# Turning batch 0's queries behind both probes of the first token, with small products among the warming ones

## The chip, the cores and the metric

The kernel runs on one core of a Trainium2 chip. The metric is the device time of one execution in microseconds (us), where lower is better. Times of the kernel before are the median of three runs; the profile comes from one further execution.

## What is computed

Eight batches, eight heads, 576 tokens, head width 64. First, 32 packs per head attend to the keys and values, and the queries then attend to the packed result; second, each batch's tokens go through a two-layer expert network (512 to 1024 to 512 wide), whose expert is chosen by a gate:

```python
def sm_attn(qq, kk, vv):
    s = scale * np.matmul(qq, kk.transpose(0, 1, 3, 2))
    a = np.exp(s - np.max(s, axis=-1, keepdims=True))
    a = a / (np.sum(a, axis=-1, keepdims=True) + 1e-09)
    return np.matmul(a, vv)
p_packed = sm_attn(p, k, v)
x = sm_attn(q, p_packed, p_packed)        # heads side by side: (8, 576, 512)
# per token: expert e by argmax of x @ w_gate, or the one before it by w_local
h = np.maximum(x[b, s] @ w1[e], 0.0)
out[b, s] = p[e] * (h @ w2[e])
```

## The kernel before

The kernel takes one expert for a whole batch, that of its first token, and works through the eight batches one behind the other; other experts, where a token has strayed, are done by a general branch at the end. For each batch the packs and keys (`turn_keys`) and queries (`turn_queries`) are turned so that the head width lies on the partitions, `scores` and `keys` compute the packed attention, and `queries` (for batch 0 `first_queries`) the second attention. `pack_weights` multiplies the expert's first-layer weights by the packed values (line 1190), so that layer 1 (`layer1`, line 1218) works on the attention shares directly; a product in single precision is split into a high and a low half on each side (wph and wpl, a2h and a2l, h and its rest, w2s) and done in three parts. Layer 2 (`layer2`, line 1271) adds up eight chunks of 128 hidden units for five blocks of tokens: three products make one group of a block and a chunk.

Batch 0 has a way of its own, since nothing is there to hide it. Before any load is there, `keep_warm` issues products on zeros (line 228), five of 256 columns by the list `WARM`, and more of them wherever the planner sees TensorE wait before the first layer. Packs are turned (line 425), then keys (line 451, six groups of three turns of 128 columns), then the packs' scores are taken (line 459). When the two halves of the packed values (ppT) are there, `early_choice` finds the expert of the first token alone: two probes (line 987, one per half of the heads), an exponential on ScalarE (line 1004), the turned shares on VectorE (et, line 1011), and their product with the gate (line 1020), which needs the gate weights that line 950 makes and line 959 copies on ScalarE. Its largest entry is the expert; SyncE reads it into a register, and only then are this expert's weights loaded: w1k (the first half of layer 1 in two pieces), four pieces of layer 2, and w1t, the second half of layer 1. The queries of batch 0 (load at line 292, turned at line 451, copied out of PSUM at line 452 by ScalarE, one of six by VectorE) are needed for the second attention of all its tokens, at line 459 again.

What order all this takes is set by a planner (`weave`): every stage is a generator that yields `need(...)`, a condition on tiles, banks of PSUM and flags; `Clock` estimates when each is ready; and the first thread that is ready by that estimate is let on, the layers' thread (`chunks`) behind the others. The order is fixed when the program is built, and each engine then runs its own list in order. So a condition that changes at one place also moves what the planner puts into the stretch behind it. A bank of PSUM is handed out by `bank`, the one that is free soonest.

## Time and profile before

| | us |
|---|---|
| median of 3 runs | 407.37 |
| lowest and highest of these | 407.05, 409.86 |
| the profiled execution | 410.66 |
| its span, first to last instruction | 408.9 |

The five engines are TensorE (PE, its weight loads apart as PEld), VectorE (DVE), ScalarE (ACT), GpSimd (POOL) and SyncE (SP, which issues the loads). A timeline row gives the start, the time that it covers, and the count of its instructions; products in fp32 stand there as two passes each, those of the layers as one. In the order's rows below, a product counts once.

### The profile page before, as it was taken

The numbers are of one execution on the slowest core, as the hardware profiler recorded it, in microseconds if no ns is written. First come the engines' busy times: TensorE is split into PE (matmuls) and PEld (weight loads), VectorE is DVE, ScalarE is ACT, GpSimd is POOL, SyncE is SP. The second block draws the span as 40 slices with busy tenths as digits, with TensorE's granted clock in tenths as the row PEclk, the third lists the DMA queues.
The fourth block names the chain that finished last, engine by engine and source line by source line (L and its number), as shares of the span: only waits on it lengthen the run. The fifth ranks groups of instructions, "written<-read, shape, count | busy, mean of one in ns | idle before, by whom it ended". The sixth has DMA issues, their size and how long they took to land.

```text
span 408.9 us, 10974 instructions
## 1 busy us (share of the span) xinstructions
PE 396.4 (97%) x4267; PEld 318.3 (78%) x4268; DVE 263.1 (64%) x755; ACT 179.8 (44%) x423; POOL 110.2 (27%) x139
## 2 busy tenths in 40 slices
PE   8888999999999999999999999999999999999994
PEld 7656877788786888778877788778878788778883
DVE  3677657778788877576776688439863695332221
ACT  2564733644337642294315741545343642453121
POOL 1006600812036313054303521234303422323000
PEclk9999999999999999999999999999999999999998
DMA  7889799990999999849996996699693104910102
GB/s 221 247 281 271 108 132 334 205 222 27 154 249 276 232 148 214 320 145 165 181 313 219 162 195 228 240 171 174 151 328 113 65 0 138 325 44 22 54 0 70
DMA packets 183133, 73.02 MB, mean 179 GB/s; under 512 B 158949, under 2 KB 162085, under 8 KB 182949
## 3 DMA queue, kind: packets, MB, share of 16 engines
q1 hardware_dynamic: 182932, 72.15, 74.2%
q8 instruction: 35, 0.57, 0.6%
q14 instruction: 22, 0.17, 0.1%
q10 hardware_dynamic: 144, 0.13, 0.1%
HBM read 62.82 MB, written 9.44 MB: 177 GB/s over the span
## 4 chain that ended last, share of the span: by engine, by line
PE 89%; DMA 6%; SPq 1%; DVE 1%; issue 1%; ACT 0%; ACTq 0%
PE bank L1271 44%; PE bank L1218 25%; PE bank L1275 4%; PE bank L1190 4%; PE bank L1279 4%; DMA w1t<-in_moe_w_dram 3%; DMA raw<-in_q_dram 2%; PE bank L569 2%; PE bank L764 2%; PE bank L521 2%; DMA raw<-in_k_dram 1%; PE bank L1039 1%; SPq L1149 1%; PE bank L587 0%; DVE wpl L1202 0%
## 5 line engine op out<-in xcount | busy, mean ns | idle before, releaser
L1271 PE MATMUL bank<-w2s,h 128*128 128x512 f32 (+1 forms) x792 | 202.1, 390 | 0.0
L1271 PEld LDWEIGHTS bank<-w2s,h 128*128 128x128 f32 x792 | 138.3, 188 | 28.0 <-issue 4.0
L1250 POOL TENSOR_TENSOR w2s<-w2raw,w2s 128x512 fp32r<-128x512 f32 (+1 forms) x68 | 83.3, 1244 | 146.9 <-ACT w2s L1246 114.5
L1233 DVE SCALAR_TENSOR_TENSOR h<-bank,h 128x256 fp32r<-128x256 f32 x192 | 61.1, 347 | 80.7 <-ACT h L1229 80.4
L1229 ACT ACTIVATE h<-bank 128x320 fp32r<-128x320 f32 (+1 forms) x128 | 52.7, 412 | 126.3 <-PE bank L1218 125.6
L1218 PEld LDWEIGHTS bank<-a2h,wph 128*128 128x128 f32 x256 | 46.1, 188 | 18.2 <-issue 5.9
L1218 PE MATMUL bank<-a2h,wph 128*128 128x256 f32 (+1 forms) x256 | 56.8, 303 | 0.0
L1218 PE MATMUL bank<-a2h,wpl 128*128 128x256 f32 (+1 forms) x256 | 55.0, 296 | 0.2 <-DVE wpl L1202 0.2
L1218 PE MATMUL bank<-a2l,wph 128*128 128x256 f32 (+1 forms) x256 | 55.0, 296 | 0.0
L1246 ACT CAST w2s<-w2raw 128x512 fp32r<-128x512 f32 x64 | 39.0, 619 | 8.9 <-DMA w2raw<-in_moe_w_dram 8.5
L1218 PEld LDWEIGHTS bank<-a2h,wpl 128*128 128x128 f32 x256 | 41.0, 188 | 0.4 <-DVE wpl L1202 0.4
L1218 PEld LDWEIGHTS bank<-a2l,wph 128*128 128x128 f32 x256 | 40.9, 189 | 0.0
L827 POOL TENSOR_TENSOR a2l<-a2t,a2h 128x320 fp32r<-128x320 f32 (+1 forms) x26 | 20.7, 817 | 65.7 <-ACT a2h L821 65.7
L1202 DVE TENSOR_TENSOR wpl<-bank,wph 128x512 fp32r<-128x512 f32 (+1 forms) x34 | 21.2, 652 | 13.4 <-ACT wph L1199 13.3
L1199 ACT CAST wph<-bank 128x512 fp32r<-128x512 f32 (+1 forms) x34 | 17.4, 566 | 22.3 <-PE bank L1190 22.2
L1275 PE MATMUL bank<-w2s,h 128*128 128x512 f32 x64 | 25.9, 404 | 0.0
L1279 PE MATMUL bank<-w2s,h 128*64 128x512 f32 x64 | 25.2, 393 | 0.0
L1310 ACT ACTIVATE o<-bank,pe 128x512 f32<-128x512 f32 x23 | 15.5, 700 | 12.4 <-PE bank L1271 12.4
L751 DVE STREAM_TRANSPOSE qn<-qn 128x1152 f32<-128x1152 f32 x14 | 19.0, 1363 | 0.0
L1190 PE MATMUL bank<-w1t,ppT 64*32 64x512 f32 x240 | 16.3, 601 | 1.6 <-DMA w1t<-in_moe_w_dram 1.6
L472 DVE STREAM_TRANSPOSE qn<-qn 128x1152 f32<-128x1152 f32 x12 | 16.2, 1353 | 0.0
L1275 PEld LDWEIGHTS bank<-w2s,h 128*128 128x128 f32 x64 | 12.0, 188 | 5.3 <-issue 3.2
(166 smaller groups left out, 382.7 us busy)
## 6 DMA issues: line engine op xcount, KB each, us to landing
w2raw<-in_moe_w_dram SPq DMA_DIRECT2D x64, 256.0 KB, 7.7
w1t<-in_moe_w_dram SPq DMA_DIRECT2D x15, 1024.0 KB, 7.1
qn<-in_q_dram SPq DMA_DIRECT2D x28, 288.0 KB, 4.5
out_dram<-o SPq DMA_DIRECT2D x31, 256.0 KB, 2.5
kv<-in_v_dram SPq DMA_DIRECT2D x24, 288.0 KB, 6.5
qn<-in_k_dram SPq DMA_DIRECT2D x24, 288.0 KB, 4.6
raw<-in_k_dram SPq DMA_DIRECT2D x4, 576.0 KB, 4.8
kv<-in_v_dram SPq DMA_DIRECT2D x4, 560.0 KB, 9.5
```

The source lines that it names most:

```text
L751: nc.vector.transpose(out=qT, in_=qT)
L827: engine.tensor_tensor(out=a2l[:, cols], in0=a2t[:, cols], in1=a2h[:, cols].bitcast(F32), op=ALU.subtract)
L1190: nc.tensor.matmul(out=ts[Q][32 * h:32 * h + 32, :width], lhsT=packs_of(st, rows, Q, h), rhs=w1t[rows, h], start=True, stop=True,)
L1202: nc.vector.tensor_tensor(out=lo[:, Q, cols], in0=ts[Q][:, :width], in1=hi[:, Q, cols].bitcast(F32), op=ALU.subtract,)
L1218: nc.tensor.matmul(out=t[:, :width], lhsT=st["wp"][c // 4][wi][:, Q, fs], rhs=a2[ai][Q][:, ts], start=(n == 0), stop=(n == 5),)
L1229: nc.scalar.activation(out=h[:, :n], in_=t[:, :n], func=AF.Relu)
L1233: nc.vector.scalar_tensor_tensor(out=h[:, dst:dst + z - a], in0=t[:, a:z], scalar=0.0, in1=h[:, a:z].bitcast(F32), op0=ALU.max, op1=ALU.su ...
L1246: nc.scalar.copy(out=w[:, 0], in_=raw)
L1250: rest.tensor_tensor(out=w[:, 1, cols], in0=raw[:, cols], in1=w[:, 0, cols].bitcast(F32), op=ALU.subtract)
L1271: nc.tensor.matmul(out=acc, lhsT=hs[hi], rhs=w[:, wi, cols], start=(c == 0 and n == 0), stop=(c == NC - 1 and n == 2),)
L1275: nc.tensor.matmul(out=acc, lhsT=h[:, EDGE:EDGE + 2 * TAIL], rhs=w[:, 0], start=(c == 0), stop=False, skip_group_check=True,)
L1279: nc.tensor.matmul(out=acc[0:TAIL], lhsT=h[:, EDGE:EDGE + TAIL], rhs=w[:, 1], start=False, stop=(c == NC - 1), skip_group_check=True,)
```

## The change

The list `WARM` loses one of its five wide products, and twenty-nine products of 32 columns on 64 rows come ahead of it, on the four column groups of the array in turn. `turn_queries` of batch 0 waits until both probes are issued, not only the first. Everything else that moves is moved by the planner.

```diff
--- before.py
+++ after.py
@@ -42,7 +42,7 @@
 
 FIRST_BACKLOG = 1400.0
 
-WARM, FILL, EACH = (256,) * 5, 0.8, 1.8
+WARM, SHORT, FILL, EACH = (256,) * 4, 29, 0.8, 1.8
 
 LAT, SAME = 160.0, 127.0
 START, FIRST_LOAD = 6100.0, 1700.0
@@ -227,6 +227,9 @@
             at_, n = (0, n) if aside_[0] is warm_ps else (HALF, n * 7 // 8)
             nc.tensor.matmul(out=aside_[0][:, at_:at_ + n], lhsT=warm[:, :128], rhs=warm[:, :n], start=True, stop=True)
 
+    for n in range(SHORT):
+        g = 32 * (n % 4)
+        nc.tensor.matmul(out=warm_ps[g:g + 32, :32], lhsT=warm[:64, g:g + 32], rhs=warm[:64, :32], start=True, stop=True)
     keep_warm(*WARM)
     clock.until["PE"], clock.until["DMA"] = START, FIRST_LOAD
 
@@ -741,7 +744,7 @@
     def turn_queries(st, Q):
         if st["early"]:
             if Q == 0:
-                yield need(when=lambda: st.get("probed", 0) > 0)
+                yield need(when=lambda: st.get("probed", 0) > 1)
                 act, dve = nc.scalar.copy, nc.vector.tensor_copy
                 yield from turn_whole(st, "q", (act, act, act, dve, act, act))
             return
```

The first place is TensorE from the first probe of the first token on. Here `ppT,q` are the probes, `wgl,ppT` the gate weights, `ident,raw` a group of turns (of batch 0's queries down to the row with `gate`, and of batch 1's keys behind the row with `p_in`), `qT,ppT` the scores of batch 0's queries. Before:

```order
L987 MATMUL bank_124<-ppT,q_88 32x32 x4
L451 MATMUL bank_306<-ident,raw 128x128 x3
L987 MATMUL bank_124<-ppT,q_88 32x32 x4
L950 MATMUL bank_315<-wgl,ppT 32x32 x8
L228 MATMUL bank_66<-warm 128x128
L451 MATMUL bank_335<-ident,raw 128x128 x3
L451 MATMUL bank_340<-ident,raw 128x128 x3
L451 MATMUL bank_345<-ident,raw 128x128 x3
L451 MATMUL bank_350<-ident,raw 128x128 x3
L1020 MATMUL bank_124<-gate_90,et 1x32 x2
L451 MATMUL bank_361<-ident,raw 128x128 x3
L425 MATMUL bank_397<-ident,p_in 128x128 x2
```

After (all lines behind the added ones are three higher):

```order
L990 MATMUL bank_152<-ppT,q_116 32x32 x8
L953 MATMUL bank_337<-wgl,ppT 32x32 x8
L454 MATMUL bank_347<-ident,raw 128x128 x3
L454 MATMUL bank_361<-ident,raw 128x128 x3
L454 MATMUL bank_366<-ident,raw 128x128 x3
L454 MATMUL bank_372<-ident,raw 128x128 x3
L454 MATMUL bank_377<-ident,raw 128x128 x3
L454 MATMUL bank_382<-ident,raw 128x128 x3
L1023 MATMUL bank_152<-gate_118,et 1x32 x2
L228 MATMUL bank_66<-warm 128x128
L462 MATMUL bank_394<-qT,ppT 32x6x16x3 x4
L462 MATMUL bank_399<-qT,ppT 32x6x16x3 x4
```

The probes and gate weights stand ahead of all query turns now, the sixth group of these comes ahead of the logit product (line 1020, now 1023), and the scores of batch 0 come ahead of batch 1's packs and keys.

At the same place on ScalarE: the copies of ppT and of the query turns, the exponential of the first token (`es,em`) and the copy of the gate weights. Before:

```order
L736 COPY ppT<-bank_298 128x128
L452 COPY qT<-bank_306 128x384
L1004 ACTIVATE es,em<-es,em 128x32
L959 COPY gate_90<-bank_315 128x64
L452 COPY qT<-bank_335 128x384
L452 COPY qT<-bank_340 128x384
L452 COPY qT<-bank_350 128x384
L452 COPY qT<-bank_361 128x384
L429 COPY p_in<-bank_397 128x256
```

After:

```order
L739 COPY ppT<-bank_326 128x128
L455 COPY qT<-bank_347 128x384
L1007 ACTIVATE es,em<-es,em 128x32
L455 COPY qT<-bank_361 128x384
L455 COPY qT<-bank_366 128x384
L962 COPY gate_118<-bank_337 128x64
L455 COPY qT<-bank_377 128x384
L455 COPY qT<-bank_382 128x384
L432 COPY p_in<-bank_453 128x256
```

The first query copy stays ahead of the exponential; the gate copy goes from the row behind the exponential to the third row behind it.

The second place is TensorE around the products that need w1t. Of the layer-2 rows (`w2s,h`) two stand for each chunk, one for each of the first two token blocks: a bank for each block. Before:

```order
L1271 MATMUL bank_574<-w2s,h 128x512 x3
L1271 MATMUL bank_583<-w2s,h 128x512 x3
L1218 MATMUL bank_590<-a2h,wph 128x256 x2
L1218 MATMUL bank_590<-a2h,wpl 128x256 x2
L1218 MATMUL bank_590<-a2l,wph 128x256 x2
L1190 MATMUL bank_608<-w1t,ppT 32x512 x4
L1190 MATMUL bank_609<-w1t,ppT 32x512 x4
L1271 MATMUL bank_574<-w2s,h 128x512 x3
L1271 MATMUL bank_583<-w2s,h 128x512 x3
L1271 MATMUL bank_574<-w2s,h 128x512 x3
L1271 MATMUL bank_583<-w2s,h 128x512 x3
L1218 MATMUL bank_643<-a2h,wph 128x256 x2
```

After:

```order
L1274 MATMUL bank_600<-w2s,h 128x512 x3
L1274 MATMUL bank_609<-w2s,h 128x512 x3
L1221 MATMUL bank_616<-a2h,wph 128x256 x2
L1221 MATMUL bank_616<-a2h,wpl 128x256 x2
L1221 MATMUL bank_616<-a2l,wph 128x256 x2
L1274 MATMUL bank_600<-w2s,h 128x512 x3
L1193 MATMUL bank_641<-w1t,ppT 32x512 x4
L1193 MATMUL bank_642<-w1t,ppT 32x512 x4
L1274 MATMUL bank_609<-w2s,h 128x512 x3
L1274 MATMUL bank_600<-w2s,h 128x512 x3
L1274 MATMUL bank_609<-w2s,h 128x512 x3
L1221 MATMUL bank_676<-a2h,wph 128x256 x2
```

One group of chunk 1 has moved from behind the products of w1t to ahead of them.

At the same place on VectorE: `sT,sm` and the three rows named `sm` belong to the softmax of batch 0's other tokens, `a2t` is its result turned back, and `wpl` the low half of w1t's products. Before:

```order
L1233 SCALAR_TENSOR_TENSOR h<-bank_590,h 128x256
L884 TENSOR_REDUCE sm_438<-sT_436 128x20
L1202 TENSOR_TENSOR wpl<-bank_608,wph 128x512
L1202 TENSOR_TENSOR wpl<-bank_609,wph 128x512
L886 TENSOR_SCALAR sm_438<-sm_438 128x20
L888 RECIPROCAL sm_438<-sm_438 128x20
L890 TENSOR_TENSOR sT_436<-sT_436,sm_438 128x640
L898 STREAM_TRANSPOSE a2t<-sT_436 128x160 x4
```

After:

```order
L887 TENSOR_REDUCE sm_449<-sT_447 128x20
L1236 SCALAR_TENSOR_TENSOR h<-bank_616,h 128x256
L889 TENSOR_SCALAR sm_449<-sm_449 128x20
L891 RECIPROCAL sm_449<-sm_449 128x20
L893 TENSOR_TENSOR sT_447<-sT_447,sm_449 128x640
L1205 TENSOR_TENSOR wpl<-bank_641,wph 128x512
L901 STREAM_TRANSPOSE a2t<-sT_447 128x160 x2
L1205 TENSOR_TENSOR wpl<-bank_642,wph 128x512
L901 STREAM_TRANSPOSE a2t<-sT_447 128x160 x2
```

The rest of the softmax (lines 886 to 890) has moved ahead of the two low halves, and two of its four turns back stand between these.

## Rows read from the trace of the kernel before

**Rows 1.** The page, busy time by engine.
```profile
PE 396.4 (97%) x4267; PEld 318.3 (78%) x4268; DVE 263.1 (64%) x755; ACT 179.8 (44%) x423; POOL 110.2 (27%) x139
```

**Rows 2.** The chain that ended last, in order of time: start us, us, what.
```profile
1.88 5.11 DMA raw<-in_k_dram
7.01 10.07 DMA raw<-in_q_dram
25.53 10.35 DMA w1t<-in_moe_w_dram
...
47.66 1.39 PE bank L1271 x6
```

**Rows 3.** PE's waits, whole run: waited for, us, times, longest.
```profile
PE bank L1190 <- DMA w1t<-in_moe_w_dram: 1.6, 1, 1.6
...
PE bank L569 <- issue: 1.0, 1, 1.0
```

**Rows 4.** Stretches of 0.5 us: us, PE busy (instructions), granted clock, DMA share, GB/s.
```profile
6.50:7.00 0.50, 0.50 (x4) 1.00 0.74 248
7.00:7.50 0.50, 0.50 (x7) 1.00 1.00 348
```

**Rows 5.** Timeline, front: start, us, engine, line, out<-in, xcount [idle <-releaser].
```profile
1.31 4.63 PE L228 MATMUL bank<-warm 128*128 128x256 f32 x10 [1.31 <-DVE warm L221]
...
5.73 0.64 PE L425 MATMUL bank<-ident,p_in 128*128 128x128 f32 x2
...
17.75 0.31 PE L950 MATMUL bank<-wgl,ppT 64*32 64x32 f32 x16
```

**Rows 6.** Timeline, the choice of the first expert.
```profile
16.41 0.27 ACT L736 COPY ppT<-bank 128x128 f32<-128x128 f32 x1 [0.28 <-PE bank L733]
...
17.21 0.52 PE L451 MATMUL bank<-ident,raw 128*128 128x128 f32 x3 [0.65 <-DMA raw<-in_q_dram]
...
17.83 0.48 ACT L452 COPY qT<-bank 128x384 f32<-128x384 f32 x1 [1.15 <-PE bank L451]
...
18.23 0.32 ACT L1004 ACTIVATE es<-es,em 128x32 f32<-128x32 f32 x1
...
18.55 0.19 ACT L959 COPY gate<-bank 128x64 f32<-128x64 f32 x1
...
18.84 1.46 ACT L452 COPY qT<-bank 128x384 f32<-128x384 f32 x3
...
19.34 0.21 DVE L1011 STREAM_TRANSPOSE et<-es 128x32 f32<-128x32 f32 x1
...
19.71 0.28 PE L1020 MATMUL bank<-gate,et 128*1 128x32 f32 x4
...
21.27 1.20 PE L459 MATMUL bank<-qT,ppT 64*32 64x288 f32 x32
```

**Rows 7.** Timeline, the start of the layers and the seam.
```profile
28.80 0.67 PE L1190 MATMUL bank<-w1k,ppT 64*32 64x256 f32 x16 [1.19 <-DMA w1k<-in_moe_w_dram]
...
30.75 6.17 POOL L1250 TENSOR_TENSOR w2s<-w2raw,w2s 128x256 fp32r<-128x256 f32 x8 [12.81 <-ACT w2s L1246]
...
35.50 0.81 DVE L884 TENSOR_REDUCE sm<-sT 128x20 f32<-128x640 f32 x1
...
35.93 1.09 PE L1190 MATMUL bank<-w1t,ppT 64*32 64x512 f32 x16 [1.55 <-DMA w1t<-in_moe_w_dram]
...
36.95 3.01 PE L1271 MATMUL bank<-w2s,h 128*128 128x512 f32 x12
37.06 1.07 ACT L1199 CAST wph<-bank 128x512 fp32r<-128x512 f32 x2 [1.93 <-PE bank L1190]
37.68 1.29 DVE L1202 TENSOR_TENSOR wpl<-bank,wph 128x512 fp32r<-128x512 f32 x2 [1.36 <-ACT wph L1199]
38.88 0.17 DVE L886 TENSOR_SCALAR sm<-sm 128x20 f32<-128x20 f32 x1
...
40.26 1.03 DVE L898 STREAM_TRANSPOSE a2t<-sT 128x160 f32<-128x160 f32 x4
```

## The prediction

> **What bounds the kernel now.** I read the page's busy shares first: TensorE (PE) is busy 396.4 of 408.9 us [rows 1], so time can only come from the 12 us in which it isn't, or from work that it does for nothing. The list of who waited for whom comes next, for PE over the whole run: the longest wait for other work is 1.6 us for w1t, the second half of the first expert's layer-1 weights; the 1.0 us at line 569 has no releaser but "issue", and I can't tie it to this change [rows 3]. The chain that ended last then shows what the front hangs on: three loads, one behind the other [rows 2]. Batch 0's keys land at 6.99 (1.88 + 5.11), its queries at 17.08 (7.01 + 10.07), w1t at 35.88 (25.53 + 10.35). The queries' load is issued when the keys have landed, and SP's list of instructions is the same in both kernels, so the first two landings are fixed by the DMA engines and not by PE. The third is counted from the token's expert choice, which the weight loads wait for.

> So the change is worth what it does to three places: the choice (near 20 us), the wait for w1t (near 35 us), and the seam at 39 us where the second half of the weights is first used. Behind that PE is full, and PE's order is the same in both kernels from about row 180 of 1266 on (of the order without row numbers), so what stands gained or lost at the seam is still there at the end.

> **The warming products.** One 128x256 product is two passes in the trace; ten passes take from 1.31 to 5.73, where the packs' turn starts, 0.44 us each [rows 5]. Taking one wide product away gives 0.88 us. The 29 small ones are 58 passes. The nearest row is line 950, sixteen passes of 32 columns on four column groups in 0.31 us [rows 5]. Most of that is the last one running out, since the four passes of line 1020 take 0.28 [rows 6]; with 0.19 us for it, an estimate between these two rows, the others start 0.12 / 15 = 8 ns apart. That row runs at the high level, this stretch at the low one: PE starts 4 instructions in the half microsecond before 7.0 and 7 in the one behind it [rows 4]. [...] Bounds: 58 x 8 ns = 0.45 us if the level doesn't matter, 58 x 16 = 0.9 us if it does, and 58 x 0.44 / 8 = 3.2 us if nothing overlaps. I take 0.9: the packs' turn stays at 5.73 and the whole front where it was. At the lower bound PE comes 0.4 us early to keys that land at 6.99 and then queries that land at 17.08, which is worth nothing. At 3.2 us PE is 2.3 us late, the eighteen key turns run wholly at the high level (18 x 0.107 = 1.9 us from 8.0, ending near 9.95 instead of 8.6), and 1.3 us is passed on.

> [...]

> **The probe and the choice.** Before, the first query turn stands ahead of the second probe on PE and waits for the queries' landing: 17.21 [rows 6]. After, both probes and the gate weights go first. The second copy of the packs ends at 16.68 (16.41 + 0.27) [rows 6]; the probes and gate weights behind it take about 0.3 us, so PE reaches the query turns by 17.15 and they start at 17.21 as before. That the probe is earlier earns nothing, because ScalarE is in order and the copy of the first query turn still stands ahead of the token's exponential in its order: copy at 17.83, exponential at 18.23, both unchanged [rows 6]. What does change is the row behind: the gate copy, at 18.55 before, now stands behind two more query copies. Three of these took 1.46 us [rows 6], 0.49 each, so the gate copy moves to 18.55 + 0.97 = 19.52 and ends at 19.71. The logit product (line 1020) before started 0.16 us after the turned exponentials (19.34 + 0.21 = 19.55), at 19.71 [rows 6]. Now the gate is later than these, and the product starts at 19.71 + 0.16 = 19.87. **The choice, and with it every weight load, comes 0.2 us later.** Bounds: 0 if the copies pack tighter, 0.4 if the accumulator read of the exponential holds them back.

> The six query turns in a row save PE nothing. Batch 0's scores started at 21.27 [rows 6] behind the pack and key turns of batch 1; now they wait for the last query copy only, two copies behind the gate at 19.71 + 0.97 = 20.7, so they start near 20.9, 0.35 us earlier, and VectorE's softmax with them. This is hidden: PE stands still 1.19 us at 28.80 for the second w1k piece [rows 7], a landing that now comes 0.2 us later. Batch 1's key turns, pushed behind, fill the same stretch ahead of 28.80. So layer 1 begins 0.2 us later.

> **The wait for w1t.** Here the new order helps. Before, PE waited 1.55 us for w1t at 35.93 [rows 7] with the layer-2 products of chunk 1 queued behind it. After, one group of three of these stands ahead. Six such passes, two groups, take 1.39 us where nothing stops them [rows 2]: 0.69 us a group. Its operands are there: POOL does eight halves from 30.75 in 6.17 us [rows 7], 0.77 each, so chunk 1 is done at 33.83, or 34.0 with the delay, and PE comes to it at about 34.5. **Gain 0.69 us**, with 1 us of waiting left. Bounds: 0, if the group is itself late, and the 0.69.

> **The seam.** w1t's products start at 36.1, 0.2 late; they take 1.02 us (35.93 to 36.95), then three groups, not four: PE comes to chunk 4's layer 1 at 37.15 + 2.07 = 39.2, before at 36.95 + 4 x 0.69 = 39.7 [rows 7]. But VectorE's order has changed too: lines 886 to 890 are pulled ahead of the low halves of the new weights (line 1202), and two turns (line 898) stand between the two halves. Lines 886 to 890 took 38.88 to 40.26 [rows 7], 1.4 us; behind line 884 (35.50 + 0.81) [rows 7] plus 0.2 they end at 37.9. The first cast of ScalarE ends at 37.06 + 0.54 + 0.2 = 37.8 [rows 7], so the first half runs 37.9 to 38.5 (1.29 / 2 each), two turns to 39.05 (1.03 / 2) and the second half to 39.7 [rows 7]. PE needs it at its fourth product, 39.2 + 0.35 = 39.55, and gets it at 39.85. **A new wait of 0.3 us**, bounds 0 and 0.6. Behind it: VectorE's batch-0 softmax is 1 us earlier, which nobody waits for.

> **Sum.** + 0.2 - 0.69 + 0.3 = - 0.2 us: from the profiled execution's 410.66 (span 408.9 and 1.76 around it) to 410.5. The median of the runs shown, 407.37, lies 3.3 us under the profiled execution; the same step gives 407.2. That is far inside 1% (4.07 us), about what a measurement of this kernel can tell from no change.

> **Rivals.** *Nothing is given back.* w1t's ten microseconds are mostly the other loads that share the engines, so the landing might not follow its issue; and if VectorE is a little quicker the seam's wait is gone. Then - 0.69: 406.7. For it: 10.35 us for this load, twice the 5.11 of the keys' [rows 2]. Against it: all of these loads are counted from the choice.

> *The high level comes later.* [...] Fourteen of the eighteen key turns ran behind 7.0; at 0.213 instead of 0.107 us they cost 1.5 us more, and the four score groups of the keys (about 1.0 us) another 1.0. Of the 2.5 us, hardly 0.1 is slack ahead of the queries' turns, and the first copy, the exponential and the choice all follow: - 0.2 + 2.4 = + 2.2, 409.6, slower than before. It decides from about 0.3 us of delay at the query turns, where it eats the forecast's gain. Against it: the four wide products still run right up to the packs' turn at 5.73, as five did. [...]

> *The change doesn't do what it says.* The group is moved, but w1t's wait and the seam swallow it, and only the late choice is left: + 0.2, 407.6.

> **How the numbers follow.** Forecast 0.5, nothing given back 0.2, late level 0.15, swallowed 0.15. For the range the low end takes the full 0.69 and that the 1.0 us at line 569 isn't met again: 407.37 - 1.7 = 405.7. The high end is the late level, 409.6. More than 1% off needs 4 us, twice the largest price here, so 0.03 for faster and 0.04 for slower.

> **What would show it.** Right: line 1020 some 0.2 us later in the changed kernel, the wait for w1t about 1 us instead of 1.55 with one group of line 1271 ahead of it, a short wait of line 1218 for wpl near 39.5, and the packs' turn near 5.7. Wrong: the choice earlier than 20.0; a packs' turn behind 6.3 or key turns that are spaced at 0.21 us throughout; a new wait behind 40 us, where I count none; a total under 405.7 or over 409.6.

## The result, and the profile of the changed kernel

The changed kernel took 415.02 us in the median of six runs (412.62 to 416.22), the kernel before, in six runs (the three shown before and three beside it), 408.99 (407.05 to 410.82): a ratio of 1.0141, interval [1.0111, 1.0171]. It is slower, by more than the forecast's range allows. In a second set of runs (the first experiment) the ratio was 1.0060 [1.0027, 1.0092]. All ratios here leave out executions more than 1.5% above the fastest of the same kernel: two of the order alone and one of the changed kernel with reductions. The profiled execution after took 412.62 us with a span of 410.9, the one before 410.66 with 408.9. The first is the fastest of its six runs, the second 1.7 us over the median of its kernel's six, so this pair shows only some 2 us of the loss.

The page's busy line after, against [rows 1]: 52 more PE products, and as many more weight loads, are recorded, and PE is 2.4 us longer busy. These are 58 small passes, less 2 wide ones, less 4 filling ones that the planner leaves out in the new order: the order alone has 4,263, the warming alone 4,323.

```profile
PE 398.8 (97%) x4319; PEld 318.6 (78%) x4320; DVE 267.7 (65%) x755; ACT 179.9 (44%) x423; POOL 109.8 (27%) x139
```

PE's waits over the whole run, after. Against [rows 3], the wait for w1t is down from 1.6 to 0.7 us, line 569's 1.0 us "issue" wait is gone, and a new one of 1.5 us heads the list: line 718, the changed kernel's name for line 715 (lines behind the added ones are counted 3 higher).

```profile
PE bank L718 <- issue: 1.5, 1, 1.5
PE bank L232 <- DVE warm L221: 1.3, 1, 1.3
PE bank L1193 <- DMA w1k<-in_moe_w_dram: 1.0, 1, 1.0
PE bank L1193 <- DMA w1t<-in_moe_w_dram: 0.7, 2, 0.6
...
PE bank L1221 <- DVE wpl L1205: 0.4, 2, 0.2
PE bank L524 <- DVE qn L475: 0.3, 1, 0.3
```

The timeline of PE after: the warming, the packs' turn (L428), the packed values (L718), the choice (L1023), and the first layers.

```profile
1.31 1.06 PE L232 MATMUL bank<-warm 64*32 64x32 f32 x58 [1.31 <-DVE warm L221]
2.30 3.78 PE L228 MATMUL bank<-warm 128*128 128x256 f32 x8
5.87 0.63 PE L428 MATMUL bank<-ident,p_in 128*128 128x128 f32 x2
...
14.25 1.32 PE L718 MATMUL bank<-kv,a1T 116*32 116x64 f32 x78
17.03 0.27 PE L718 MATMUL bank<-kv,a1T 115*32 115x64 f32 x2 [1.46 <-issue]
...
18.81 2.18 PE L454 MATMUL bank<-ident,raw 128*128 128x128 f32 x18
21.29 0.28 PE L1023 MATMUL bank<-gate,et 128*1 128x32 f32 x4 [0.30 <-DVE et L1014]
...
34.44 0.86 PE L1274 MATMUL bank<-w2s,h 128*128 128x512 f32 x3
35.88 1.09 PE L1193 MATMUL bank<-w1t,ppT 64*32 64x512 f32 x16 [0.58 <-DMA w1t<-in_moe_w_dram]
...
39.33 0.62 PE L1221 MATMUL bank<-a2h,wpl 128*128 128x256 f32 x2
```

The start is as forecast: 58 small passes take 2.30 - 1.31 = 0.99 us and the packs' turn is at 5.87 [rows 5: 5.73]. Then PE does 78 of the 80 passes of line 718 and stands still for 1.46 us with no releaser. The choice follows at 21.29 [rows 6: 19.71]. Yet w1t's products start at 35.88 [rows 7: 35.93]: w1t lands no later, although the choice is 1.58 us later, and one group of line 1274 now runs ahead of the wait, as forecast. So in this pair of profiles the late front is paid for by 36 us, and the loss comes later. The next table aligns both kernels' products counted from the last one, and gives by how many us a product is later than in the kernel before (columns: times in the profile of before; the kernels are those of the experiments below).

```
                                   at 80    92   102   126   142   218   224   402
changed kernel                     -0.09 +0.45 +1.20 +1.59 +3.22 +3.70 +2.48 +2.46
warming alone                      -0.14 -0.14 -0.14 +0.22 +2.37 +2.55 +1.34 +1.29
order alone                        -0.99 -0.46 +0.30 +0.47 +1.11 +1.38 +0.89 +0.93
order alone, reductions            -1.94 -1.41 -1.41 -0.60 +0.05 +1.10 +0.56 +0.69
the same without the constant      -1.21 -1.21 -1.21 -0.97 +0.12 +0.39 -0.44 -0.33
before, reductions                 -1.71 -1.71 -1.71 -1.70 -1.95 -1.92 -1.50 -1.35
before, small products later       +1.22 +1.22 +1.22 +2.72 +4.24 +5.11 +3.90 +3.70
```

The first column of one profile can't be read by itself: the kernel before with reductions does the same work up to 92 us and stands 1.71 us earlier at 80. Over all eighteen profiles the column says more. The five with the standstill at line 718 stand between -0.14 and +2.66 there (median +0.68), the thirteen without it between -1.94 and 0.00, but for one at +1.72 (median -0.99). An estimate from these medians is that the standstill costs 1.7 us at 80 us; the profile of before is itself a late one.

### The profile page after: what moved, and what is told of

The parts are those of the page before. It is cut to its first block, busy times and chain, and to the rows that moved or that the text cites. A ratio compares the mean times of both kernels' runs of the same rounds, so it can differ in the third digit from the quotient of the medians.

```text
span 410.9 us, 11072 instructions
## 1 busy us (share of the span) xinstructions
PE 398.8 (97%) x4319; PEld 318.6 (78%) x4320; DVE 267.7 (65%) x755; ACT 179.9 (44%) x423; POOL 109.8 (27%) x139
## 4 chain that ended last, share of the span: by engine, by line
PE 79%; DVE 7%; DMA 7%; ACT 2%; issue 2%; SPq 1%; POOL 0%; DVEq 0%; ACTq 0%; POOLq 0%
PE bank L1274 37%; PE bank L1221 21%; DMA w2raw<-in_moe_w_dram 6%; PE bank L1278 3%; PE bank L1282 3%; PE bank L1193 3%; PE bank L572 2%; PE bank L767 2%; DVE swap L504 1%; PE bank L524 1%; DMA w1t<-in_moe_w_dram 1%; PE bank L228 1%; PE bank L1042 1%; DVE h L1236 1%; DVE aT L562 1%
```

## The experiments

**The parts, and PE's instruction count.** Four kernels: the changed one again; only its warming (the old condition, `probed > 0`); only its order (five wide products, no small one); and the new order with 66 small and 2.5 wide products, which puts 256 PE instructions more than before ahead of line 718. The instructions theory, as the expectations call it: PE stands still where a piece of its instructions ends inside a run of very short products and the next piece isn't there yet. The fourth kernel rests on pieces of 256, the author's estimate; the profile after gives some 250 (35 packets of the queue that its page calls "instruction", for 8,752 instructions of PE, if all of them are PE's).

```diff
-WARM, SHORT, ... = (256,) * 4, 29, ...
+WARM, SHORT, ... = (256,) * 5, 0, ...              # order alone
+WARM, SHORT, ... = (256, 256, 128), 66, ...        # 256 instructions more
```

> The changed kernel once more, beside the others. Its first profile shows PE standing still for 1.46 us ahead of the last of the 80 small passes of the packed values (line 718), with nothing named that it waits for; a packet of the instruction queue (16 KB) begins 2.4 us before it goes on. All theories: ratio 1.011 to 1.017 to before. [...]

> The warming of the changed kernel (29 small, 4 wide) with the old condition for the queries' turn. Instructions theory: 112 more PE instructions ahead of the packed values, as in the changed kernel, so the standstill of 1.4 to 1.6 us at the 79th pass of line 718 is there, and the ratio is 1.010 to 1.016. Order theory (the new order of probes, turns and softmax makes VectorE late for the batches behind): no standstill there and ratio 0.998 to 1.002. Clock theory (the small products leave PE at the low level for longer): ratio 1.010 to 1.016 too, but key turns at 0.21 us spacing behind 7.0.

> The new condition (both probes first) with the old five wide warming products. Instructions theory: the ends of the pieces stand where they stood before at line 718, no standstill there, ratio 0.996 to 1.003. Order theory: ratio 1.010 to 1.016. Clock theory: ratio 0.996 to 1.003. My blind forecast for the order alone was - 0.2 us, ratio 0.9995.

> The changed kernel with 66 small and 2.5 wide products (256, 256 and 128 columns): the same time on PE as 29 and 4 (66 x 2 x 17 ns + 2.5 x 0.85 us = 4.4 us against 1.0 + 3.4), but 256 instructions more than before ahead of the key turns instead of 112. Instructions theory: the ends of the pieces fall on the same products as in the kernel before, no standstill at line 718, ratio 0.996 to 1.004. Order theory: unchanged, 1.010 to 1.016. Clock theory: more small products, so no better than the changed kernel, 1.012 to 1.025.

Measured: 1.0060 [1.0027, 1.0092], warming alone 1.0060 [1.0034, 1.0087], order alone 1.0009 [0.9983, 1.0036], 256 more 1.0049 [1.0017, 1.0081]. The warming carries the loss. It is smaller than expected: the theory of instructions had 1.010 to 1.017 for the changed kernel and the warming alone. For 256 more instructions it had 0.996 to 1.004; 1.0049 is above that, though the interval reaches into it. The theory fits where PE stands still, as follows, but it doesn't explain what this kernel loses. The changed kernel once more and the warming alone stand still behind the same pass of line 718, by 1.38 and 0.97 us; the order alone and the kernel with 256 more do not. The first of these shows what can follow. Its rows (PE busy, granted clock behind POOL's column, DMA share, GB/s) and line 454's key turns:

```profile
16.00:18.40 2.40, 1.33 (x36) 0.82 (x35) 0.35 (x1) 0.53 (x2) 0.34 (x2) 1.00 0.74 213
18.40:22.00 3.60, 3.60 (x33) 3.56 (x26) 1.53 (x7) 1.78 (x7) 0.00 (x0) 0.53 0.53 216
22.00:24.00 2.00, 2.00 (x41) 1.06 (x39) 0.71 (x5) 0.87 (x2) 0.00 (x0) 1.00 0.00 0
```

```profile
16.73 0.27 PE L718 MATMUL bank<-kv,a1T 115*32 115x64 f32 x2 [1.38 <-issue]
...
18.51 3.85 PE L454 MATMUL bank<-ident,raw 128*128 128x128 f32 x18
```

PE stands still, resumes at 16.73, and from 18.58 to 21.99 (the trace's record of the clock) its granted clock is 0.5 (0.53 over the row from 18.40 to 22.00): the 18 turns take 3.85 us instead of 2.18 in the changed kernel's first profile, where the clock stayed up.

Why there? In the changed kernel the queue of kind "instruction" (q8 on the page) has 35 packets, 0.57 MB together and 16 KB each, and PE has 8,639 products and weight loads and 113 others. That these packets bring PE's program is inferred from the times that follow; no row says it. One of them started at 14.61 and PE went on at 17.03, 2.42 us later; with the warming alone it was 14.53 and 17.07. Counting products, weight loads and the others in the trace, PE had done 449 = 193 + 256 when it stopped in the front, and in the kernel before, near 222 us, 5,313 = 193 + 20 x 256 (packet at 219.72, 2.39 us ahead). The eighteen profiles hold 21 such waits with "issue", of 0.23 to 1.77 us. Each stands behind a count of 193 above a multiple of 256, and each ends 2.3 to 2.7 us after a packet's start.

The reading that fits, an inference: PE gets through the instructions of tiny products (78 passes of line 718 in 1.32 us) before the next packet is there. Where such a count falls into slower work no wait need follow: in the kernel before the instruction behind the 449th was the choice's first product, and PE reached it 4.5 us after the packet's start. The 29 small products are 116 instructions, the wide one 4: what follows, up to the choice, stands 112 instructions further, and behind the 449th now comes the 79th pass of line 718. The 1.0 us of line 569 [rows 3] was the same thing, and the shift took it away there: the table's fall from +3.70 to +2.48 between 218 and 224.

**That the count sets the standstill, not the small products' place.**

```diff
 # kernel before, five wide products, old condition
+late_ones()      # 29 small products behind the keys' scores, near 11 us
 # and, apart from that, four wide products and no small one:
-WARM = (256,) * 5
+WARM = (256,) * 4
```

> The kernel before, five wide products at the start and the old condition, with the 29 small products put behind the keys' scores, into the stretch of warming work near 11 to 12 us, where PE waited 0.55 us afterwards: 116 more PE instructions, the refill's end at about the 77th of line 715's 80 passes. Refill theory: a standstill of 0.9 to 1.5 us in line 715's last passes near 16 us, as in the kernel with the new warming alone; ratio 1.002 to 1.006. Theory that it is small products ahead of the first loads that cost: no standstill, ratio within 0.002 of 1. Drops of the clock: in 4 or more of 12 runs if the standstill or the number of small products brings them, in at most 2 of 12 if small products at the start do.

> The kernel before with four wide warming products instead of five and no small ones, old condition on the queries: 4 PE instructions fewer, the packs' turn 0.9 us earlier or PE idle for as long ahead of the keys. It asks whether the drops of the granted clock (a run's mean at 0.995 or under in 30 of 61 runs with small products, 9 of 136 without) go with the small products or with the missing wide one. Small-products theory: drops in at most 2 of 12 runs, no standstill in line 715, ratio 0.998 to 1.003. Missing-wide theory: drops in 4 or more of 12 runs, ratio 1.003 to 1.008.

Measured: 1.0122 [1.0080, 1.0165] and 1.0000 [0.9977, 1.0023]. Nothing of the change is in the first kernel but the 29 small products, 116 more PE instructions, at another place, and it loses as much as the changed kernel did in its first runs, more than the 1.002 to 1.006 expected. Its profile, the passes of the same line, then the stretches:

```profile
13.93 1.32 PE L727 MATMUL bank<-kv,a1T 116*32 116x64 f32 x76
17.01 0.31 PE L727 MATMUL bank<-kv,a1T 115*32 115x64 f32 x4 [1.77 <-issue]
```

```profile
16.00:18.40 2.40, 1.20 (x16) 0.75 (x16) 0.35 (x1) 0.53 (x2) 0.33 (x2) 1.00 0.77 203
18.40:22.00 3.60, 3.60 (x40) 3.22 (x40) 0.97 (x6) 1.94 (x6) 0.00 (x0) 0.53 0.54 216
```

The standstill is at the 77th pass, 4 instructions earlier than in the changed kernel, as many as the wide product that it has more, and the drop of the clock follows it again (18.48 to 21.89). The missing wide product by itself costs nothing.

**How often the clock drops.** A run's mean granted clock of 0.995 or less goes with a drop somewhere in it: the four profiles that have one stand at 0.993 to 0.995, the fourteen others at 0.996 or more. In two of the four the drop is the one above, in the two others it came near 130 and 140 us. In the five sets of runs of kernels whose profile shows the standstill at line 718 the mean was that low in 28 of 47 runs, and in each set these were 1.0 to 2.7 us longer in the median than the others. The kernels without small products, the one before among them, had it in 15 of 182. But the kernels with 66 and with fifteen small products at the start, whose profiles show no standstill in the front, had it in 7 of 20. The kernel with fifteen of them later, the last experiment, had it in none of 12. So that the standstill alone brings the drops isn't shown.

**Fewer small products.**

```diff
-WARM, SHORT, ... = (256,) * 4, 29, ...
+WARM, SHORT, ... = (256,) * 4 + (128,), 15, ...
```

> The changed kernel with fifteen small warming products (of twenty-nine) and one more wide one of 128 columns: 58 more PE instructions than in the kernel before, against 112 in the changed one. Refill theory: PE stands still where its instruction count comes to 192 above a multiple of 256 inside a burst of tiny products; with 112 more that is the 79th of the 80 passes of line 718, with 58 more it falls behind that burst, among longer products, so the pause of 1.0 to 1.5 us near 16 to 17 us goes; the drop of the granted clock near 18 to 22 us, seen in one profile behind such a pause, goes with it in nearly all runs. Median 0.5 to 1.5 us under the changed kernel's, ratio 1.001 to 1.004. Rival, the small products themselves (their kind or their duration of 17 ns a pass): half of the loss at the start stays, the pause stays, ratio as the changed kernel's 1.006. The loss between 88 and 142 us stays under both.

Measured: 1.0079 [1.0051, 1.0108]. The profile shows what was expected, no standstill, and the time does not (1.001 to 1.004 was expected): a miss. Three more profiles, of this kernel and of the one with 256 more instructions, were to show what their longer executions hold:

> A further single look at the kernel with 66 small products and 256 more PE instructions than before. Standstill theory: an execution above 411.5 us shows a standstill of over 0.5 us in the front and may show a drop of the clock behind it. Clock theory: it shows a drop without a standstill. Late-landing theory: it shows neither, and a wait of PE for weights of over 1 us or held operations between 120 and 140 us.

> The same kernel once more, with the same three possibilities.

> A further single look at the kernel with fifteen small products at the start. Its first profile passed the refill's end at 17.28 us, 2.75 us behind the packet, with no standstill. Standstill theory: an execution above 412 us stands still there, in the products of lines 953 to 990, by 0.3 to 1 us, and may drop its clock behind it. Late-landing theory: as for the other two.

None stands still in the front. 411.43 us: the clock rises only at 8.72, and the keys' scores start at 10.49 instead of 9.47. 412.87 us: it rises at 8.73, and w1t is waited for by 1.43 us at 36.80, the probabilities of line 676 by 1.18 at 46.51. 413.55 us (fifteen small ones): four held operations of VectorE between 131 and 136, as below, PE waiting 0.82 us at 136.88, then the clock's drop from 140.03 to 143.45. So part of what small warming products cost at the start may be a later rise of the clock in some executions (4.2 to 7.5 us in the nine profiles without them at the start, 4.9 to 8.7 in the nine with them), and part lies far behind the front. Neither was tested apart from the rest.

**VectorE held by POOL.** In the changed kernel VectorE and POOL at 94 us, then the same in the kernel before:

```profile
94.83 2.82 DVE L504 COPY swap<-low 32x4 f32<-32x4 f32 x4
...
94.91 2.54 POOL L1253 TENSOR_TENSOR w2s<-w2raw,w2s 128x512 fp32r<-128x512 f32 x2 [8.23 <-ACT w2s L1249]
```

```profile
92.42 1.29 POOL L1250 TENSOR_TENSOR w2s<-w2raw,w2s 128x512 fp32r<-128x512 f32 x1 [2.94 <-ACT w2s L1246]
...
94.39 1.74 DVE L501 COPY swap<-low 32x4 f32<-32x4 f32 x4
...
94.47 1.29 POOL L1250 TENSOR_TENSOR w2s<-w2raw,w2s 128x512 fp32r<-128x512 f32 x1 [0.75 <-ACT w2s L1246]
```

A copy of 32x4 takes 0.16 us. One that starts beside POOL's subtraction takes 1.22 in the median and ends within 0.03 us of it, in all 43 cases of the eighteen profiles. The new order puts two casts of ScalarE, and so two subtractions of POOL, next to each other: two copies are held, not one. In the traces a small reduction beside POOL takes 0.12 to 0.20 us, as alone. So the six operations were written as reductions, with every engine's order left as it was:

```diff
-nc.vector.tensor_copy(out=y[32 * g:32 * g + 32], in_=x[o:o + 32])
+nc.vector.tensor_reduce(out=x[32 * g:32 * g + 32, :, 1], in_=x[o:o + 32, :, 0:1], op=ALU.min, axis=AX.X)
 # four copies in a loop; the two minima, low and nb, likewise
```

> The changed kernel, with the six operations between the scores' minima and the exponential's bias (two minima of 128x4, four copies of 32x4 that swap partition groups) written as reductions along the free axis; the order on every engine stays. In the profiles so far such an operation takes 0.16 us alone and 1.09 to 1.25 us when POOL's 128x512 subtraction of line 1253 runs: it ends within 0.03 us of the subtraction's end. Reductions of the same size beside POOL take what they take alone (0.19 us). Held-operations theory: the three to five held ones between 88 and 142 us take 0.2 us or less, PE's loss of 3.3 us against the kernel before in that stretch falls to 1.5 us or less, and the median falls by 1.5 to 3 us against the changed kernel (ratio near 1.000 instead of 1.006). Rival, later landings of raw layer-2 weights or another cause: the reductions are held too, or they are not held and PE still loses 3 us there; ratio 1.005 to 1.008. Standstill theory of the front: the pause of 1.0 to 1.5 us in line 718's products near 16 to 17 us is still there, since the number of PE's instructions is that of the changed kernel.

> The kernel before with the same six operations as reductions. Held-operations theory: its profile showed three held operations between 94 and 133 us (1.10 to 1.22 us each), its other executions spread over 6 us; so it gains 0.5 to 1.5 us in the median (ratio 0.996 to 0.999) and the spread of its executions shrinks. Rival: no gain, same spread. No standstill near 16 us; a pause near 222 us in line 569 (0.99 us in the profile before) stays, since PE's instructions are those of the kernel before.

> The new condition on the queries with the old five wide warming products, and the six operations as reductions. Held-operations theory: the front's gain of about 1 us, seen in the profile of the same order with the copies (offset of -0.99 us at 80 us), is kept to the end: 1 us under the kernel before with reductions, ratio 0.993 to 0.997. Rival: the order is worth nothing or is lost behind 88 us in another way: ratio equal to that of the kernel before with reductions, within 0.002. Against the changed kernel with reductions this one shows the price of the small products alone: 1 to 2 us by the standstill theory, nothing by a theory that puts the loss on the order.

Measured: the changed kernel with reductions 1.0018 [0.9988, 1.0048], the kernel before with them 0.9979 [0.9957, 1.0001], the order alone with them 0.9963 [0.9940, 0.9986]. So the warming costs 0.0055 here too, beside 0.0060 and 0.0051 in the first experiment: 2.1 to 2.5 us in all three pairs, and the standstill is still there in the first of these (1.10 us). The copies, now in the last one:

```profile
92.99 0.64 DVE L503 TENSOR_REDUCE low<-low 32x4 f32<-32x4 f32 x4
...
93.06 2.56 POOL L1252 TENSOR_TENSOR w2s<-w2raw,w2s 128x512 fp32r<-128x512 f32 x2 [8.24 <-ACT w2s L1248]
```

0.64 us for four beside the same two subtractions. The table's step between 92 and 102, 0.75 us in all eight profiles with the new order and the copies, is gone (-1.41 and -1.41). The changed kernel's ratio falls from 1.0060 to 1.0018, the direction and size expected, though the two intervals still overlap; its profiled execution waited 3.21 us for w1t at 130.05, with a clock drop behind, so its stretch behind 122 us can't be read. That the loss between 88 and 142 us would shrink to 1.5 us or less did not hold: the order alone with reductions still loses 2.0 (0.54 at 88 us, 0.80 with a w1t wait of 0.70 at 122.80, the rest behind 126, not followed further), the kernel before with reductions none. So the held copies are 0.75 us of it, not all. With reductions, the new order and the old one can't be told apart.

**The step near 88 us.** The step is 0.52 to 0.55 us in the twelve profiles of the new order that keep all of VectorE's operations, and missing in the five of the old. VectorE and PE in the changed kernel:

```profile
81.39 1.02 DVE L1068 TENSOR_TENSOR under<-lt,gmx 128x40 f32<-128x40 f32 x1
...
85.50 0.67 DVE L1092 TENSOR_SCALAR gsm<-gsm 128x5 f32<-128x5 f32 x1
...
88.44 1.34 DVE L475 STREAM_TRANSPOSE qn<-qn 128x1152 f32<-128x1152 f32 x1
```

```profile
89.04 0.47 PE L524 MATMUL bank<-qn,p_in 64*32 64x144 f32 x16
89.83 1.02 PE L524 MATMUL bank<-qn,p_in 64*32 64x144 f32 x48 [0.31 <-DVE qn L475]
```

In the kernel before the first two of these took 0.19 and 0.15 us, for there POOL was idle beside them, and the second stood behind the first transposition of the keys:

```profile
82.58 0.19 DVE L1065 TENSOR_TENSOR under<-lt,gmx 128x40 f32<-128x40 f32 x1
...
87.31 0.15 DVE L1089 TENSOR_SCALAR gsm<-gsm 128x5 f32<-128x5 f32 x1
```

```profile
79.30 2.53 POOL L1250 TENSOR_TENSOR w2s<-w2raw,w2s 128x512 fp32r<-128x512 f32 x2
84.72 1.29 POOL L1250 TENSOR_TENSOR w2s<-w2raw,w2s 128x512 fp32r<-128x512 f32 x1 [2.89 <-DVE o L1306]
```

First they were given another form, then one was left out:

```diff
-nc.vector.tensor_tensor(out=under, in0=lg, in1=mx..., op=ALU.subtract)
+nc.vector.scalar_tensor_tensor(out=under, in0=lg, scalar=0.0, in1=mx..., op0=ALU.add, op1=ALU.subtract)
-nc.vector.tensor_scalar(out=sm, in0=sm, scalar1=1e-9, scalar2=None, op0=ALU.add)
+nc.vector.scalar_tensor_tensor(out=sm, in0=sm, scalar=1e-9, in1=sm, op0=ALU.add, op1=ALU.max)
 # second kernel: the addition of 1e-9 left out, the rest as with reductions
```

> The new condition with five wide products and the six operations of the scores as reductions, and also the two of the expert choice that were still held beside POOL's subtraction: the difference from the maximum (128x40, 1.02 us held, 0.19 alone) and the sum's small constant (128x5, 0.67 held, 0.15 alone), each as an operation with a scalar and a second tensor (0.19 us beside POOL in the one case seen). Held-operations theory: both take 0.2 us, the second transposition of the keys near 87 us ends 0.8 to 1.3 us earlier, PE's wait of 0.30 us for it near 88 us (0.54 us of offset with the spacing) goes; median 0.3 to 0.8 us under the version with only the six, ratio 0.992 to 0.996. Rival: still held in the new form, or another operation is; no change (0.996).

> The new condition with five wide products, the six operations of the scores as reductions, and the addition of 1e-9 to the gate's sum of exponentials left out (the sum holds an exponential of zero, so it is at least 1): one vector operation less per batch, 0.66 us beside POOL's subtraction near 85 us. PE's order stays. Held-operations theory: the second transposition of the keys near 87 us ends 0.7 us earlier against PE, the wait of 0.30 us near 88 us and the 0.54 us of offset go; ratio 0.993 to 0.997. Rival: the transposition is late for another reason (the landing of the keys, the relu work): wait stays.

Measured: 0.9999 [0.9979, 1.0019]: a miss, for the new forms were held as well:

```profile
81.17 1.02 DVE L1067 SCALAR_TENSOR_TENSOR under<-lt,gmx 128x40 f32<-128x40 f32 x1
...
85.28 0.66 DVE L1093 SCALAR_TENSOR_TENSOR gsm<-gsm 128x5 f32<-128x5 f32 x1
```

With these forms held, this kernel should run as the order alone with reductions did, which had 0.9963 in another set of runs. So a difference of 0.3% between two sets says little here. Without the addition 0.9981 [0.9960, 1.0002], and the wait is gone, in one row of 64 passes:

```profile
84.48 1.34 DVE L475 STREAM_TRANSPOSE qn<-qn 128x1152 f32<-128x1152 f32 x1
86.40 1.34 DVE L475 STREAM_TRANSPOSE qn<-qn 128x1152 f32<-128x1152 f32 x1
```

```profile
87.92 1.26 PE L523 MATMUL bank<-qn,p_in 64*32 64x144 f32 x64
```

The table has -1.21 on both sides of it. This kernel's median is 408.97 us beside 410.26 of the kernel before, though its interval reaches 1.0002.

**Moving the packets' ends on purpose.** Fifteen small products behind the keys' scores, on top of the kernel with the two new forms:

> The last one with fifteen small products behind the keys' scores: 60 more PE instructions, so that the refill's end that stood still in line 568's products near 222 us (0.5 to 1.4 us) falls 60 instructions earlier there, and the one near 16 us behind line 717's passes. Refill theory: neither standstill, PE 0.5 to 1.4 us earlier behind 222 us; ratio 0.990 to 0.995, if these few small products do not bring clock drops. Rival: the standstill near 222 us stays or moves to another burst, ratio as without them or up to 0.002 above.

Measured: 0.9989 [0.9965, 1.0014], short of the 0.990 to 0.995 expected and beside 0.9999 for the same kernel without the fifteen, and no clock of 0.995 or less in twelve runs. The standstill near 222 us is gone as expected; two others came, 0.62 us at 17.95 and 1.02 at 262.78. In every one of the eighteen profiles PE stands still at one or more counts of 193 above a multiple of 256.

## Why the prediction was wrong

**The failed step: the term for the small products, put at nothing.** The sum took them as time ("I take 0.9"), which the wide product taken away gives back. As time that was right: 0.99 us, or 17 ns a pass instead of 16. The 16 is the forecast's 8 ns doubled, and no run shows it as such: beside the 17 ns the runs show 15 with 66 of them (132 passes from 1.31 to 3.27), and in the kernel before key turns 0.213 us apart up to 7.01 and 0.11 from 7.15 on. What they measured instead is a loss of 2.1 to 2.5 us in three pairs of kernels with and without them. The sum never counted that they are 116 instructions, so that every later count of 193 above a multiple of 256 meets another product. In the changed kernel that is a standstill of 1.46 us at line 718, some 1.7 us at 80 us by the estimate above, and an execution whose clock drops loses more. This isn't the whole price: with fifteen or 66 small products at the start no profile stands still in the front, and the loss is 0.5 to 0.8% all the same. The row that shows the standstill was in hand, and was put aside: "the 1.0 us at line 569 has no releaser but "issue", and I can't tie it to this change". The range's low end even counted that it might not be met again, but not that it might be met elsewhere.

**The order, right in the front and not followed far enough.** With the order alone the logit product came at 19.83 (forecast 19.87; first row), and the new wait for wpl at 39.09 was 0.62 (forecast 0.3, bound 0.6; second row):

```profile
19.83 0.58 PE L1023 MATMUL bank<-gate,et 128*1 128x32 f32 x4 [0.30 <-DVE et L1014]
...
39.09 0.39 PE L1221 MATMUL bank<-a2h,wpl 128*128 128x256 f32 x1 [0.62 <-DVE wpl L1205]
```

The first number is in part luck: the product was released by the turned exponentials (et) and not by the gate copy, as the sum had it. One group of line 1271 did run ahead of w1t's products, before a wait of 0.58 us in the changed kernel and no wait in the order alone. But "what stands gained or lost at the seam is still there at the end" failed too. It was argued from PE's order alone, the same from row 180 on (in the traces from 78 us on). VectorE's and ScalarE's orders differ up to some 90 us, and by short operations that came to stand beside POOL's subtractions PE lost 0.54 + 0.75 = 1.3 us in all eight profiles of the new order with the copies, where the forecast had counted a gain of 0.2. "VectorE's batch-0 softmax is 1 us earlier, which nobody waits for" leaves out the same question, beside whose work an earlier engine's work then stands. That the changed kernel's profile is at -0.09 us at 80 us, near the forecast's - 0.2, is luck.

**The rivals.** "Nothing is given back" fits the first pair of profiles, where w1t came no later for a choice 1.58 us later. That its landing doesn't follow the choice isn't shown: in the nine profiles in which PE waited for w1t, its products started at 34.2 to 37.6 us, with the choice at 19.1 to 22.3, on the whole later with a later choice. "The high level comes later", 0.15, was the nearest: it named the slower side and a price of 2.4 us for the clock. It had the wrong moment in the changed kernel's profile (the rise was at 6.93, before at 7.05), though the 66 small ones showed a late rise twice. "The change doesn't do what it says" did not occur. The chance of 0.04 for slower rested on "twice the largest price here"; the largest price was not among those listed. The range also hung on a median of three runs, 407.37: in the four later sets the unchanged kernel's own median was 409.62 to 410.28, above the range's top of 409.6.

**What stays open.** Why the clock falls behind some standstills (two of the profiles, 1.38 and 1.77 us) and not behind others (three at line 718, 0.97, 1.10 and 1.46, and 1.42 near 221 us in the kernel before with reductions), and why it fell once near 140 us behind no such standstill. Why the two kernels with small products at the start and no standstill in the front of their profiles still lose 0.5 to 0.8%: late rise, held operations and landings were each seen, in a profile or two, and how they share it was not measured. So the rival that the small products cost something by what they are, beside their count, stands; a kernel that moves PE's count by other instructions than products was not run. The first six runs' 1.0141 and the later 1.0060 of the same kernel have intervals that don't meet; their share of runs with a drop (4 of 6, two of them at 0.989, against 6 of 10, none under 0.992) points the way, without being settled.

## What to carry to other kernels

Count instructions as well as time: with 29 tiny products more, 0.99 us on PE and 116 instructions, the 0.99 us "issue" wait of line 569 near 222 us was gone and one of 1.46 us stood at line 718 near 17 us. All 21 such waits stood in a burst of tiny products or, but for one, just behind one; look where the shift puts the next. When an order changes, compare all engines to the row where they agree again, and look for short VectorE operations that come to stand beside a long POOL operation: here a 32x4 copy took 1.22 us beside POOL's subtraction and 0.16 alone, a reduction of that size 0.16 (four in 0.64 us), so write such operations as reductions where a form of them exists. And read a loss from several profiles: one execution of the same work was 1.7 us ahead of another by 80 us.
